# Inverse sums of the exponentials: turned once as 16 columns, stored to DRAM and loaded back spread over partitions; first T one slot later

## The chip, the cores and the metric

The kernel runs on one core of one Trainium2 chip. The metric is the device time of one execution in microseconds; lower is better. The profiler's times are microseconds from the start of the span unless marked ns. Its engines are PE (TensorE's matmuls), PEld (its weight loads), DVE (VectorE), ACT (ScalarE), POOL (GpSimd) and SP (SyncE, which issues the DMAs).

## The reference

A transformer block for 2048 tokens of 1024 features: a layer norm that is scaled and shifted by the row c, causal attention in four segments of 512 tokens with a running memory, an output projection, a second norm, and a gated feed-forward layer. The part that the change touches is the attention of one head (32 heads of 32 features):

```python
for s in range(N):                       # N = 4 segments of L = 512 tokens
    logits = einsum("bhqd,bhkd->bhqk", qs, ks) * scale + mask
    p = softmax(logits, axis=-1)
    a_dot = einsum("bhqk,bhkd->bhqd", p, vs)
    pq = phi(qs)
    num = einsum("bhld,bhde->bhle", pq, M)
    den = einsum("bhld,bhd->bhl", pq, z)[..., None] + 1e-6
    o = g * (num / den) + (1.0 - g) * a_dot
    M = M + einsum("bhld,bhle->bhde", phi(ks), vs)
    z = z + einsum("bhld->bhd", phi(ks))
```

The softmax divides by a sum of exponentials for each token and head, and the result is weighted with 1 − g. That factor, (1 − g) / sum, is what the change carries another way.

## The kernel before, in words

Everything is float32; projections are three products of rounded high and low parts. After a start of some 95 us the attention runs as 32 steps, one for each group of four heads (G = 8) and each segment, two segments of every group in a first half and two in a second. The feed-forward layer follows from some 1020 us on and is not touched.

The steps are pipelined in a loop (n from 0 to 32). Each loop is a list of slots, the string ORDER, in which every letter takes one piece of a generator: K (v and k of the next step: four pieces of v, then k, then the turns vT and kT), Q (q of the next step), S (scores of this step, query block by query block), A (sums of the running memory), M (what is read from the memory), V (the values of the step before), N (norm of later tokens, in the loops n = 1 to 9 or so). TensorE runs in exactly this order. DVE, ACT, POOL and SP are ordered by a scheduler with a cost model, and each of them then takes its instructions strictly in the order given.

For one step the work is:

- S: four products for each block of 128 queries, S (L498). DVE finds the row minimum of the negated scores (L500, mm) and ACT the exponentials with their sums (L502, ll). Then mt, a turn by DVE (tt, L513) and four writes into qs (L515) put the row maxima into the operand of the next product.
- the inverse sums: rc, 128 queries by 16 (four query blocks by four heads), is the reciprocal of ll (L519) times 1 − g (L520). ACT copies it to rx, with each value repeated over the 32 features of its head (L522).
- V: four key blocks. T(kc) is four products of keys with queries (L562), one for each head; ACT takes the exponentials pt (L564) and POOL sets what the mask excludes to zero (L565). PV(kc) sums them with the values vx into O (L571). The slots are T(0), T(1), PV(0) and PV(1), T(2), T(3), PV(2) and PV(3), then the end.
- the end: O holds features by tokens, so the factor must stand as features by tokens too. TensorE turns rx in four 128 x 128 blocks into the PSUM tile R (L585), ACT copies it (L589), DVE multiplies O with it (L590). Where a memory exists, ry is turned the same way (Y, L585) and added (L593). The result goes to DRAM (oT_d, L595).

PSUM has two buffers for projections (v, k and q in turn), five that S, T, num, R and Y share, and one for O. vr (L369) is the copy of v, kh (L384) the high part of k, eq, ql and pq come from q. na (L245) is the normalized row block of N, with mra (L243) and rsa (L238) ahead of it, and hta (L272) its turned and scaled form.

Of the kernel before, what the change touches and what calls it, by code (L numbers as in the profile page):

```python
# [19 lines left out]
P = 128  # L20
# [16 lines left out]
def block_kernel(ctx: ExitStack, tc: tile.TileContext, x, c, wmod, wq, wk, wv, wo, beta, wg, wu, wd, out):  # L37
# [10 lines left out]
    x1_d = dram.tile([T, D], F32, name="x1_d")  # L48
    mix_d = dram.tile([4 * L, L], F32, name="mix_d")
# [437 lines left out]
    def scores(n, g, s):  # L487
# [5 lines left out]
        for i in range(4):  # L493
            nk = max(256, (i + 1) * P)
            nv = (i + 1) * P
            for j in range(4):
                ps = s_ps(f"S{nm}_{j}{i}")
                nc.tensor.matmul(ps[:, :nk], qs[:96, j, i * P:(i + 1) * P], ks[:96, j, :nk], start=True, stop=True)  # L498
                sj = t2(f"sj{nm}_{j}{i}", "sj", bufs=3)
                nc.vector.tensor_tensor_reduce(out=sj[:, :nv], in0=ps[:, :nv], in1=mask[:, L - nv:], scale=-1.0,  # L500
                                               scalar=3.4e38, op0=ALU.add, op1=ALU.min, accum_out=mm[:, j, i:i + 1])
                nc.scalar.activation(sj[:, :nv], sj[:, :nv], AF.Exp, bias=mm[:, j, i:i + 1], scale=-1.0,  # L502
                                     accum_out=ll[:, i, j:j + 1])
            if i < 3:
                yield
# [14 lines left out]
        nc.vector.tensor_mul(rc, rc, omg[:, 4 * g:4 * g + 4].unsqueeze(1).to_broadcast([P, 4, 4]))  # L520
        rx = t2("rx" + nm, "rx", shape=(P, 4, 4, DH))
        nc.scalar.activation(rx, rc.unsqueeze(3).to_broadcast([P, 4, 4, DH]), AF.Copy)  # L522
        SC[n] = [rx, None]
# [25 lines left out]
    def values(n, g, s):  # L549
        nm = f"{g}_{s}"  # L550
        qs, ks, vx, pq = ST.pop(n)
        rx, ry = SC.pop(n)
# [21 lines left out]
        for kc in (0, 2):  # L574
            for k in (kc, kc + 1):
                T(k)
                yield
# [4 lines left out]
        def turned(r, name):  # L582
            ps = s_ps(name + nm)
            for i in range(4):
                nc.tensor.transpose(ps[:, i * P:(i + 1) * P], r[:, i].rearrange("p a b -> p (a b)"), ident)  # L585
            return ps

        rr = tmp_tile("R" + nm)
        nc.scalar.activation(rr, turned(rx, "R"), AF.Copy)  # L589
        nc.vector.tensor_mul(rr, po, rr)  # L590
        yield
        if s > 0:
            nc.vector.tensor_add(rr, rr, turned(ry, "Y"))  # L593
# [730 lines left out]
    ORDER = "K N K K V K V N K K V V K N V K S Q S V V Q S Q A S K M Q V V"  # L1324
# [6 lines left out]
    with tc.manual_schedule(engines={mybir.EngineType.PE}):  # L1331
# [27 lines left out]
        for n in range(len(steps) + 1):  # L1359
# [22 lines left out]
            if n == 30:  # L1382
# [5 lines left out]
                def cut(k):  # L1388
# [3 lines left out]
                         (22, lambda: get(2)), (32, lambda: cut(2)), (26, lambda: get(3)), (35, lambda: cut(3))]  # L1392
# [69 lines left out]
```

## Time and profile before

| what | value |
|---|---|
| time, median of three runs | 2802.66 us (2799.39 to 2803.0) |
| the profiled execution: time | 2800.21 us |
| its span, mean granted clock | 2798.5 us, 0.995 |
| TensorE busy in the span | 2727.7 us, 97% |
| attention loops, 100 to 1020 us | 920 us; PE 905.49, ACT 655.32, DVE 593.80, POOL 340.83 busy |
| share of the DMA engines in that stretch | 0.60, 132 GB/s |

A row of the windows gives, for a stretch, the busy time of each engine with its count of instructions in brackets. A row of the groups gives line, engine, operation, tiles and shapes, then the busy time and the mean ns of one, then the idle time of the engine just before them with what ended it. A row of the waits names who waited for what, with the total, the number and the longest. In the timeline a row is start, length, engine, line and a count of like instructions in a row; brackets hold the idle time before it. The chain of waits names the work that ended last at each moment.

### The profile page before, as it was taken

The numbers are of one execution on the slowest core, as the hardware profiler recorded it, in microseconds if no ns is written. First come the engines' busy times: TensorE is split into PE (matmuls) and PEld (weight loads), VectorE is DVE, ScalarE is ACT, GpSimd is POOL, SyncE is SP. The second block draws the span as 40 slices with busy tenths as digits, with TensorE's granted clock in tenths as the row PEclk, the third lists the DMA queues.
The fourth block names the chain that finished last, engine by engine and source line by source line (L and its number), as shares of the span: only waits on it lengthen the run. The fifth ranks groups of instructions, "written<-read, shape, count | busy, mean of one in ns | idle before, by whom it ended". The sixth has DMA issues, their size and how long they took to land.

```text
span 2798.5 us, 38460 instructions
## 1 busy us (share of the span) xinstructions
PE 2727.7 (97%) x13276; PEld 2207.4 (79%) x13276; DVE 1761.9 (63%) x3727; ACT 1291.8 (46%) x2861; POOL 540.9 (19%) x986
## 2 busy tenths in 40 slices
PE   5999999999999999999999999999999989999999
PEld 4777777777777777888888887888888878888887
DVE  7566566766666744677776768666777744334543
ACT  6688876767676735234343224222322243232220
POOL 0333334333332531100000002000000002112432
PEclk9999999999999999999999999999999999999999
DMA  7566655665555647655555644334576675544652
GB/s 228 129 148 137 159 113 127 149 140 125 116 115 99 144 171 242 202 207 211 214 205 186 243 177 152 127 137 151 188 250 246 248 259 168 182 143 153 206 187 79
DMA packets 229604, 480.17 MB, mean 172 GB/s; under 512 B 17440, under 2 KB 92192, under 8 KB 229408
## 3 DMA queue, kind: packets, MB, share of 16 engines
q1 hardware_dynamic: 229408, 477.72, 56.7%
q8 instruction: 104, 1.70, 0.3%
q14 instruction: 92, 0.75, 0.1%
HBM read 300.96 MB, written 126.35 MB: 153 GB/s over the span
## 4 chain that ended last, share of the span: by engine, by line
PE 87%; DVE 7%; issue 2%; DMA 2%; ACT 2%; POOL 1%; SPq 0%; DVEq 0%; ACTq 0%; POOLq 0%
PE f L1125 37%; PE d L1284 19%; PE k L365 6%; PE q L365 5%; PE y L630 5%; PE v L365 3%; PE S L498 3%; PE O L571 3%; PE T L562 3%; DVE qs L515 1%; PE M L478 1%; PE R L585 1%; DVE sj L500 1%; PE num L536 1%; PE vT L378 0%
## 5 line engine op out<-in xcount | busy, mean ns | idle before, releaser
L1125 PE MATMUL f<-A,B 128*128 128x512 f32 x4704 | 1074.6, 390 | 4.9 <-DVE c L1090 3.2
L1125 PEld LDWEIGHTS f<-A,B 128*128 128x128 f32 x4704 | 882.3, 188 | 190.5 <-issue 2.9
L1284 PE MATMUL d<-wb,ah 128*128 128x512 f32 x2352 | 536.0, 390 | 7.3 <-DVE wb L1174 3.8
L1284 PEld LDWEIGHTS d<-wb,ah 128*128 128x128 f32 x2352 | 442.3, 188 | 101.0 <-DVE wb L1174 4.9
L500 DVE CUSTOM_DVE_ANT_0 sj<-S,mask 128x384 f32<-128x384 f32 (+3 forms) x512 | 227.9, 487 | 183.9 <-PE S L498 175.3
L502 ACT ACTIVATE sj<-sj,mm 128x384 f32<-128x384 f32 (+3 forms) x512 | 282.4, 556 | 27.5 <-DVE mm L500 25.2
L564 ACT ACTIVATE pt<-T 128x256 f32<-128x256 f32 (+3 forms) x512 | 184.9, 455 | 119.9 <-PE T L562 119.2
L1174 DVE TENSOR_TENSOR ah<-ar,ah 128x1792 fp32r<-128x1792 f32 x56 | 115.9, 2070 | 183.9 <-ACT ah L1173 183.9
L565 POOL TENSOR_SCALAR_AFFINE_SELECT pt<-pt 128x128 f32<-128x128 f32 x512 | 165.7, 342 | 339.1 <-ACT pt L564 332.1
L1173 ACT ACTIVATE ah<-ar 128x1792 fp32r<-128x1792 f32 x56 | 95.3, 1702 | 275.5 <-PE d L1284 245.9
L1092 ACT ACTIVATE g<-g 128x512 f32<-128x512 f32 x56 | 35.4, 632 | 309.9 <-DVE g L1092 309.9
L201 POOL TENSOR_TENSOR w<-r,w 128x256 fp32r<-128x256 f32 x180 | 133.8, 774 | 162.4 <-ACT w L196 162.3
L763 DVE TENSOR_TENSOR B<-t,B 128x512 fp32r<-128x512 f32 x168 | 116.1, 691 | 56.4 <-ACT B L766 56.3
L1197 POOL TENSOR_TENSOR yo<-u,gbb 128x256 f32<-128x256 f32 x32 | 29.2, 937 | 559.0 <-DMA hid_d<-sc 556.8
L766 ACT ACTIVATE B<-t 128x512 fp32r<-128x512 f32 x168 | 105.5, 628 | 63.2 <-PE f L1125 59.7
L630 PE MATMUL y<-wo,hho 128*128 128x512 f32 x384 | 125.8, 393 | 0.0
L562 PE MATMUL T<-qs,ks 128*128 128x256 f32 (+2 forms) x512 | 114.5, 338 | 5.6 <-DVE qs L515 1.9
L562 PEld LDWEIGHTS T<-qs,ks 128*128 128x128 f32 x512 | 83.2, 188 | 45.6 <-issue 21.7
L1089 ACT ACTIVATE g<-f 128x512 f32<-128x512 f32 x56 | 33.5, 599 | 176.8 <-PE f L1125 176.8
L763 DVE TENSOR_TENSOR B<-rg,B 128x512 fp32r<-128x512 f32 x112 | 77.8, 695 | 53.0 <-ACT B L766 52.9
L498 PE MATMUL S<-ks,qs 96*128 96x256 f32 (+2 forms) x512 | 108.1, 332 | 1.2 <-DVE mm L500 1.2
L1215 POOL TENSOR_TENSOR xo<-xo,yo 128x256 f32<-128x256 f32 x64 | 69.6, 1115 | 195.5 <-DMA xo<-x_d 155.4
(232 smaller groups left out, 4338.3 us busy)
## 6 DMA issues: line engine op xcount, KB each, us to landing
ar<-hid_d SPq DMA_DIRECT2D x56, 896.0 KB, 5.2
rg<-wg SPq DMA_DIRECT2D x56, 512.0 KB, 4.6
ru<-wu SPq DMA_DIRECT2D x56, 512.0 KB, 5.5
hid_d<-g SPq DMA_DIRECT2D x56, 512.0 KB, 3.0
sc<-hid_d SPq DMA_DIRECT2D x56, 512.0 KB, 5.6
hid_d<-sc SPq DMA_DIRECT2D x56, 512.0 KB, 3.0
br<-wT_d SPq DMA_DIRECT2D x49, 512.0 KB, 5.9
qs<-qh SPq DMA_DIRECT2D x64, 256.0 KB, 4.8
```

The lines of the kernel that those rows point to most:

```text
L201: eng.tensor_sub(w[:, 1, k:k + 256], r[:, k:k + 256], f32(w[:, 0, k:k + 256]))
L365: nc.tensor.matmul(ps, w[:, a], b, start=(kt == 0 and a == 0 and b is hi), stop=(kt == KT - 1 and a == 1))
L498: nc.tensor.matmul(ps[:, :nk], qs[:96, j, i * P:(i + 1) * P], ks[:96, j, :nk], start=True, stop=True)
L500: nc.vector.tensor_tensor_reduce(out=sj[:, :nv], in0=ps[:, :nv], in1=mask[:, L - nv:], scale=-1.0, scalar=3.4e38, op0=ALU.add, op1=ALU.min ...
L502: nc.scalar.activation(sj[:, :nv], sj[:, :nv], AF.Exp, bias=mm[:, j, i:i + 1], scale=-1.0, accum_out=ll[:, i, j:j + 1])
L562: nc.tensor.matmul(ps[:, :nn], ks[:, j, kc * P:(kc + 1) * P], qs[:, j, L - nn:], start=True, stop=True)
L564: nc.scalar.activation(pt, ps[:, nn - n:nn], AF.Exp)
L565: nc.gpsimd.affine_select(pt[:, :P], pt[:, :P], pattern=[[1, P]], compare_op=ALU.is_ge, fill=0.0, base=0, channel_multiplier=-1)
L630: nc.tensor.matmul(ps, b[:, i * P:(i + 1) * P], w[:, a, g % 2], start=(g == 0 and a == 0 and b is hi), stop=(g == G - 1 and a == 1))
L763: eng.tensor_sub(dst[:, k], a[:, k], b[:, k])
L1125: nc.tensor.matmul(ps, B[m, i][:, a, kt * P:(kt + 1) * P], A[p, i, kt][b], start=(start and kt == 0 and a == 0 and b == 0), stop=(kt == 3 ...
L1284: nc.tensor.matmul(ps[t], ops[n][:, x, k, t * P:(t + 1) * P], b[:, y, kk % 2], start=(kk == 0 and x == 0 and y == 0), stop=(kk == 13 and x ...
```

## The change

Four things change. The inverse sums keep their 16 columns (in the order head, query block) and are no longer repeated by ACT. Right behind T(0), one turn by TensorE makes 16 rows of 128 of them; ACT copies these to 16 rows of the tile tt, and SP stores them to DRAM as 16 x 128 (rc_d, two in turn). Behind T(2), four DMAs load them back, each a row of 512 tokens repeated over the 32 partitions of a head, into the tile rr. DVE multiplies O with rr as before. The four turns and the copy at the end go; those of ry stay. The string ORDER is rearranged around T(0) and T(1), and in loop 30 the loads and cuts of two weight blocks of wo come earlier.

```diff
+    rc_d = [dram.tile([16, P], F32, name=f"rc{i}_d") for i in range(2)]
...
-                                     accum_out=ll[:, i, j:j + 1])
+                                     accum_out=ll[:, j, i:i + 1])
...
-        nc.vector.tensor_mul(rc, rc, omg[:, 4 * g:4 * g + 4].unsqueeze(1).to_broadcast([P, 4, 4]))
-        rx = t2("rx" + nm, "rx", shape=(P, 4, 4, DH))
-        nc.scalar.activation(rx, rc.unsqueeze(3).to_broadcast([P, 4, 4, DH]), AF.Copy)
-        SC[n] = [rx, None]
+        nc.vector.tensor_mul(rc, rc, omg[:, 4 * g:4 * g + 4].unsqueeze(2).to_broadcast([P, 4, 4]))
+        SC[n] = [rc, None, tt]
...
                 T(k)
+                if k == 0:
+                    ps = s_ps("R" + nm)[:16, :P]
+                    nc.tensor.transpose(ps, rc.rearrange("p a b -> p (a b)"), ident)
+                    rows = tt[:16]
+                    nc.scalar.activation(rows, ps, AF.Copy)
+                    nc.sync.dma_start(rc_d[n % 2], rows)
+                if k == 2:
+                    rr = t2("R" + nm, "rx")
+                    for j in range(4):
+                        nc.sync.dma_start(rr[32 * j:32 * j + 32], bass.AP(tensor=rc_d[n % 2].tensor, offset=rc_d[n % 2].offset + j * L,
+                                                                         ap=[[0, 32], [1, L]]))
                 yield
...
-        rr = tmp_tile("R" + nm)
-        nc.scalar.activation(rr, turned(rx, "R"), AF.Copy)
         nc.vector.tensor_mul(rr, po, rr)
...
-    ORDER = "K N K K V K V N K K V V K N V K S Q S V V Q S Q A S K M Q V V"
+    ORDER = "K N K K K V K N V K V V K N V K S Q S V V Q S Q A S K M Q V V"
...
-                         (22, lambda: get(2)), (32, lambda: cut(2)), (26, lambda: get(3)), (35, lambda: cut(3))]
+                         (16, lambda: get(2)), (24, lambda: cut(2)), (21, lambda: get(3)), (30, lambda: cut(3))]
```

TensorE in loop 25, from T(0) to the first product of O, before. A name's digits are the segment, then head and block.

```order
L562 MATMUL T_2_30_9805<-qs_2_9392,ks_174 128x512
L365 MATMUL v_2_9769<-hhh_4_0_6031,w_1_5_9536 128x512
...
L365 MATMUL v_2_9769<-hhh_4_1_6048,w_1_5_9536 128x512
L562 MATMUL T_2_01_9826<-qs_2_9392,ks_174 128x384
...
L365 MATMUL k_2_9846<-hhh_1_0_5781,w_1_5_9621 128x512
...
L365 MATMUL k_2_9846<-hhh_2_1_5880,w_1_5_9621 128x512
L378 MATMUL vT_2_9859<-ident,vr_2_9816 128x128 x4
L571 MATMUL O_2_9789<-pt_2_00_9792,vx_2_9103 32x512
```

The same place in the changed kernel:

```order
L366 MATMUL v_2_9769<-hhh_4_1_6050,w_1_5_9545 128x512
L561 MATMUL T_2_00_9800<-qs_2_9392,ks_176 128x512
...
L578 MATMUL R_2_9820<-ident,rc_2_9718 16x128
L366 MATMUL k_2_9830<-hhh_1_0_5770,w_1_5_9630 128x512
...
L561 MATMUL T_2_01_9837<-qs_2_9392,ks_176 128x384
...
L366 MATMUL k_2_9830<-hhh_2_0_5854,w_1_5_9630 128x512
...
L379 MATMUL vT_2_9863<-ident,vr_2_9795 128x128 x4
L570 MATMUL O_2_9799<-pt_2_00_9802,vx_2_9082 32x512
```

All of v now stands ahead of T(0), the first piece of k between T(0) and T(1), and one piece of k instead of two between T(1) and O.

ACT in loop 6, one of those with the norm of later tokens, before:

```order
L522 ACTIVATE rx_1_2738<-rc_1_2735 128x512
L196 ACTIVATE w_0_4_3035<-r_0_4_2880 128x1024
L564 ACTIVATE pt_1_00_2821<-T_1_00_2819 128x512
...
L369 ACTIVATE vr_1_2845<-v_1_2785 128x512
L245 ACTIVATE na_2563<-na_2563,mra_2800,rsa_2797 128x1024
L564 ACTIVATE pt_1_01_2851<-T_1_01_2849 128x384
...
L564 ACTIVATE pt_1_31_2866<-T_1_31_2864 128x384
L272 ACTIVATE hta_0_2870<-tpa_0_2869,modT 128x128 x4
```

And in the changed kernel:

```order
L370 ACTIVATE vr_1_2824<-v_1_2785 128x512
L563 ACTIVATE pt_1_00_2831<-T_1_00_2829 128x512
L563 ACTIVATE pt_1_10_2836<-T_1_10_2834 128x512
L246 ACTIVATE na_2572<-na_2572,mra_2800,rsa_2797 128x1024
L563 ACTIVATE pt_1_20_2841<-T_1_20_2839 128x512
L563 ACTIVATE pt_1_30_2846<-T_1_30_2844 128x512
L580 ACTIVATE tt_1_2728<-R_1_2849 16x128
L273 ACTIVATE hta_0_2861<-tpa_0_2860,modT 128x128 x4
L563 ACTIVATE pt_1_01_2875<-T_1_01_2873 128x384
```

vr stands ahead of the exponentials of T(0), na ahead of two of them, and the copy tt and four hta ahead of those of T(1). In every second one of these loops na stands behind all four exponentials of T(0).

DVE in loop 25, around the product with O, in the changed kernel (before, that product L590 stood between the first and the second reduce of the block of 384):

```order
L501 ISA sj_3_33_10049,mm_3_9940<-S_3_33_10047,mask 128x512
L501 ISA mm_3_9940 128x1
L592 TENSOR_TENSOR R_2_9897<-O_2_9799,R_2_9897 128x512
L509 CAST mt_3_10052<-mm_3_9940 128x16
L539 TENSOR_SCALAR dn_3_10089<-num_3_0_10083 128x8
L510 TENSOR_TENSOR mt_3_10052<-mm_3_9940,mt_3_10052 128x16
L539 TENSOR_SCALAR dn_3_10089<-num_3_1_10084 128x8
L514 STREAM_TRANSPOSE tt_3_10055<-mt_3_10052 32x32 x4
```

The product now stands behind the last reduce of S and ahead of mt and the turn.

More of the change, by code (lines that the diff above doesn't have):

```diff
@@ L551, in values @@
         qs, ks, vx, pq = ST.pop(n)
-        rx, ry = SC.pop(n)
+        rc, ry, tt = SC.pop(n)
         po = o_ps("O" + nm)
@@ L580, in values @@
             yield
[L582 to L586, printed above, removed]
-        rr = tmp_tile("R" + nm)
-        nc.scalar.activation(rr, turned(rx, "R"), AF.Copy)
         nc.vector.tensor_mul(rr, po, rr)
@@ L592, in values @@
         if s > 0:
-            nc.vector.tensor_add(rr, rr, turned(ry, "Y"))
+            ps = s_ps("Y" + nm)
+            for i in range(4):
+                nc.tensor.transpose(ps[:, i * P:(i + 1) * P], ry[:, i].rearrange("p a b -> p (a b)"), ident)
+            nc.vector.tensor_add(rr, rr, ps)
             yield
```

## The prediction

> **What bounds the kernel now.** First the page: the busy times of the engines and the chain of work that ended last.
>
> ```profile
> PE 2727.7 (97%) x13276; PEld 2207.4 (79%) x13276; DVE 1761.9 (63%) x3727; ACT 1291.8 (46%) x2861; POOL 540.9 (19%) x986
> PE 87%; DVE 7%; issue 2%; DMA 2%; ACT 2%; POOL 1%; SPq 0%; DVEq 0%; ACTq 0%; POOLq 0%
> ```
>
> TensorE is busy 97% of the span and holds 87% of the chain. The change lies in the attention loops alone, so I read the table of windows next, for the 32 loops that turn R (the first turn stands at 114.4, the last at 1008.4).
>
> ```profile
> 100.00:1020.00 920.00, 905.49 (x5226) 708.34 (x5226) 593.80 (x1978) 655.32 (x1854) 340.83 (x760) 1.00 0.60 132
> ```
>
> In these 920 us TensorE is busy 905.49, at a granted clock of 1.00; it sits idle 14.5 us. So the stage has two things to give: TensorE's own work, and at most 14.5 us of waits. ACT (655.32) and DVE (593.80) have slack as totals. What the waits are, the list of waits of PE in this window says (line waited for: us in total, times, longest):
>
> ```profile
> PE k L365 <- ACT vr L369: 3.4, 7, 0.5
> PE T L562 <- DVE qs L515: 1.9, 3, 0.8
> PE T L562 <- DVE ry L544: 1.8, 5, 0.4
> PE T L562 <- ACT pt L564: 1.4, 3, 0.8
> PE O L571 <- POOL pt L565: 1.2, 2, 1.0
> ...
> PE k L365 <- DVE pq L419: 0.7, 2, 0.3
> ```
>
> Four of these rows, k on vr, k on pq, T on qs and T on ry, are the ones that the new order touches: 3.4 + 0.7 + 1.9 + 1.8 = 7.8 us.
>
> **1. The four turns of R leave TensorE.** The timeline of PE around one of them (start, us, count), and the chain of waits at the same place with the turn of Y and one K slot:
>
> ```profile
> 802.30 0.86 PE L571 MATMUL O<-pt,vx 128*32 128x256 f32 x16
> 803.09 0.66 PE L585 MATMUL R<-ident,rx 128*128 128x128 f32 x4
> 803.50 0.48 PE L365 MATMUL q<-hhh,w 128*128 128x512 f32 x1
> 803.82 0.39 PE L365 MATMUL q<-hlh,w 128*128 128x512 f32 x1
> ```
>
> ```profile
> 798.64 1.39 PE k L365 x6
> ...
> 803.15 0.59 PE R L585 x4
> ...
> 811.43 0.44 PE Y L585 x4
> ```
>
> From R's start to the next q are 803.50 − 803.09 = 0.41 us, and that q takes 0.48 instead of 0.39, 0.09 more: 0.50 us for a loop. The chain puts 0.59 on it. 32 loops: −16.0 us by the first, −18.9 by the second. I take −16.0, since starts are recorded and ends are modelled.
>
> **2. One turn of 16 columns comes.** It is one matmul against the identity where there were four. A quarter of the chain's R row is 0.59 / 4 = 0.15 us, a quarter of its Y row 0.11; alone it can't cost more than a whole transpose by itself:
>
> ```profile
> L585 PE MATMUL R<-ident,rx x128: 272/273/330, 114.4 to 1008.4; 128*128 128x128 f32 x128
> L571 PEld LDWEIGHTS O<-pt,vx 128*32 128x32 f32 x1024 | 28.0, 109 | 38.8 <-issue 20.6 <-POOL pt L565 8.0 <-POOL hlh L224 0.2
> L585 PEld LDWEIGHTS R<-ident,rx 128*128 128x128 f32 x128 | 13.6, 142 | 7.0 <-DVE mm L500 5.2 <-issue 1.6 <-DVE hho L223 0.2
> ```
>
> So 32 x 0.15 = +4.8 us, between 32 x 0.11 = 3.5 and 32 x 0.273 = 8.7. Its weight load has 16 columns; the nearest row is the 32-column load of O at 109 ns, against 142 ns at 128 columns, so little of the load's cost goes away and I keep 0.15. [...]
>
> Terms 1 and 2 together: −11.2 us, from −18.9 + 3.5 = −15.4 to −16.0 + 8.7 = −7.3.
>
> **3. Copies and the product.** Two copies leave ACT in each loop and a small one comes; the product stays on DVE:
>
> ```profile
> L522 ACT ACTIVATE rx<-rc 128x512 f32<-128x512 f32 x31 | 19.5, 628 | 45.7 <-DVE rc L520 45.7
> L589 ACT ACTIVATE R<-R 128x512 f32<-128x512 f32 x32 | 18.5, 578 | 3.1 <-PE R L585 3.1
> L564 ACT ACTIVATE pt<-T 128x128 f32<-128x128 f32 x128 | 25.4, 288 | 14.6 <-PE T L562 13.9 <-POOL pt L565 0.6
> ```
>
> ACT loses 19.5 + 18.5 = 38.0 us and gains 32 x 0.29 = 9.3 (the 128-element exponential is the nearest row). With 265 us of slack in the stage that is worth nothing by itself. Its places count: rx stood ahead of the exponentials of T(0), and the copy of the turned R among those of S. I give it 0 here; part of it returns in term 4.
>
> **4. Waits that go.** T(0) moves one K slot back, 1.39 us by the row of k above. The waits of T on ry were 0.4 at most and those on qs 0.8 at most, less than that slot; so 1.9 + 1.8 go, unless the chain on DVE grows. It doesn't by count: the product R takes a place among the reduces of S, in a later one than before. The k that opens the new slot follows T(0) and its turn, and vr now stands ahead of T(0)'s exponentials on ACT, so 3.4 + 0.7 go as well, if v's copy (0.63) is over by the end of T(0), some 1.1 us. I take all 7.8; between 0 (each wait only moves) and all 14.5 that TensorE sits idle.
>
> **5. Waits that come.** In eight early loops the norm of later tokens runs beside the attention, and ACT takes its place in a queue. One of these loops, in the timelines of ACT and PE:
>
> ```profile
> 248.06 1.25 ACT L245 ACTIVATE na<-na,mra,rsa 128x1024 f32<-128x1024 f32 x1 [1.91 <-DMA qs<-ql]
> 249.21 1.61 ACT L564 ACTIVATE pt<-T 128x384 f32<-128x384 f32 x4
> 250.69 1.53 ACT L272 ACTIVATE hta<-tpa,modT 128x128 f32<-128x128 f32 x4
> ```
>
> ```profile
> 245.35 0.86 PE L562 MATMUL T<-qs,ks 128*128 128x384 f32 x4
> 249.73 0.66 PE L378 MATMUL vT<-ident,vr 128*128 128x128 f32 x4 [0.33 <-ACT pt L564]
> 250.32 1.81 PE L571 MATMUL O<-pt,vx 128*32 128x512 f32 x16
> ```
>
> na stood idle for 1.91 us, and the exponentials of T(1), whose products had begun at 245.35, came only behind it: ACT works in order. In the new order the queue between na and those exponentials gains the copy tt (0.29) and four hta (1.53). From na's end at 249.31: 249.31 + 0.29 + 1.53 + 1.61 = 252.7, and POOL's select of some 0.34 makes 253.1. O's last four products of this half want it about 1.7 into its 1.81, at 252.0: 1.1 us late. Where na stands ahead of two exponentials of T(0) as well, 1.03 more: 2.2. Over eight loops 1.1 gives 8.8 and 2.2 gives 17.6. But na itself comes sooner in half of them, since POOL's rsa now stands ahead of the selects; there I halve it: +7, between 0 and 17.6. In the other 24 loops ACT has, from the end of v, 0.63 (vr) + 2.06 + 0.29 + 1.61 = 4.6 us of work and POOL 0.34 behind it, 4.9; TensorE comes to the same exponentials after T(0) 1.07, the turn 0.15, a K slot 1.39, T(1) 0.86, a K slot 1.39, vT 0.44 and half of O 0.9, at 6.2. That is a cover of 1.3 us, so I set them at 0. The rows of ACT, PE and POOL that aren't above, the third that of a copy ahead of the exponentials of T(0) there:
>
> ```profile
> 788.86 2.06 ACT L564 ACTIVATE pt<-T 128x512 f32<-128x512 f32 x4
> 790.78 0.63 ACT L369 ACTIVATE vr<-v 128x512 f32<-128x512 f32 x1
> 787.85 0.60 ACT L416 ACTIVATE eq<-q 128x512 f32<-128x512 f32 x1 [2.69 <-DVE ql L411]
> 243.08 1.07 PE L562 MATMUL T<-qs,ks 128*128 128x512 f32 x4
> 794.03 0.44 PE vT L378 x4
> L565 POOL TENSOR_SCALAR_AFFINE_SELECT pt<-pt 128x128 f32<-128x128 f32 x512 | 165.7, 342 | 339.1 <-ACT pt L564 332.1
> ```
>
> **6. The round trip.** Per loop SP gets five more DMAs: one of 8 KB to DRAM and four loads of 64 KB. Nearest rows (KB each, median us to landing), SP's issue after the k copy, and the last reduce of S in that loop:
>
> ```profile
> ks<-kl SPq DMA_DIRECT2D x30, 256.0 KB, 6.8
> qs<-ql SPq DMA_DIRECT2D x30, 256.0 KB, 4.2
> hT_d<-hta SPq DMA_DIRECT2D x16, 256.0 KB, 2.6
> ...
> 800.69 1.21 SPq L395 DMA_DIRECT2D ks<-kh  x2
> ...
> 809.84 0.69 DVE L500 CUSTOM_DVE_ANT_0 sj<-S,mask 128x512 f32<-128x512 f32 x1
> ```
>
> The store follows T(0) at some 3 us and lands 2.6 to 6.8 us later, before k is copied. In nine of the loops the loads stand behind the first ks, in the others ahead of it; at some 0.6 us for an issue the last is out at 803.7 and lands at 807.9 (4.2) to 810.5 (6.8). The product R stands there behind the last reduce in five of the nine, which ends at 810.5, and up to three reduces sooner in the others. So it is just covered: cost 0, with 0 to 2.6 us to spare in the five. Behind the product on DVE are mt, the turn tt and qs, and T(0) waits for qs; behind the waiting loads on SP are ks, qs and weights, wanted only a loop later. If the cover is gone, each us past it costs up to a us of each of the nine loops, once T(0)'s own slot (1.39) is used up. [...]
>
> At the last attention loop but one, wo's loads and cuts go 5 to 8 slots earlier; O's waits on POOL there are 1.2 us in total, so I set this at 0 within ±1.2.
>
> **Sum.** −11.2 − 7.8 + 7 = −12.0. The profiled run took 2800.21 us, with a span of 2798.5: 2788.2. The three runs were 2799.39 to 2803.0 with their median 2.45 above the profiled one, so the profile lies in their lower half; I say 2788.
>
> **The rivals.**
>
> *A, the queue on ACT costs in full.* Term 5 at its upper end: −11.2 − 7.8 + 17.6 = −1.4, 2799. For it: the row of na, where exponentials waited behind it. Against: DVE and POOL bring na sooner in half the loops. [...]
>
> *B, the time comes back as waits.* The 0.35 us that terms 1 and 2 save in a loop only brings TensorE sooner to qs, which DVE's chain times; 7.8 us of waits grow by 11.2 instead of going. The change then does not do what it says: 2800. For it: T waits for qs and ry already. Against: these were 8 waits in 32 loops, and T(0) comes 1.39 later.
>
> *C, O waits for ACT in every loop: slower.* Between T(1) and O stand one K slot and vT where N, K, K and vT stood in the early loops and two K slots in the late ones. If ACT comes to vr 2.3 us after v ends (weight cuts or late exponentials of S ahead of it), the cover of 1.3 is gone and O waits 1.0 in the 24 loops, and term 5 is at its upper end: −11.2 − 7.8 + 17.6 + 24 = +22.6, 2823. Past 2808 it goes at 0.4 us for each of those loops, from 1.7 us of lateness on. For it: eq waited for ql on ACT just ahead of T(0)'s exponentials. Against: in the loop shown the exponentials of T(0) start at 788.86, and with rx gone from ahead of them they could start 0.63 sooner.
>
> *E, the load of R is late: slower.* In nine loops the last of the four loads lands 11.5 us after its issue at 803.7, 4.7 past the reduces; 1.39 is covered and 3.3 reach T(0): 9 x 3.3 = 30, 2788 + 30 = 2818. It decides at 10.4 us from the issue. For it: no row of this trace is a load that repeats one row over 32 partitions. Against: 6.8 is the slowest of the medians.
>
> *D, more waits go.* Terms 1 and 2 as taken, all 14.5 us of idling gone and nothing new: 2800.2 − 25.7 = 2774.5. Against: O on POOL and T on pt are not touched by the order.
>
> **How the numbers follow.** Forecast 0.55, D 0.15, A 0.09, B 0.07, C 0.09, E 0.05. About 0.2%, 5.6 us, is what a measurement of this kernel can tell from no change, counted from the median of 2802.66: faster means below 2797.1. Faster: forecast and D, 0.70. Same: A and B, 0.16. Slower: C and E, 0.14. The forecast's own range is 2777 to 2796 (net turns −15.4 to −7.3, waits some ±5). The range leaves out C, E and a little of D below 2772, and takes in A and B with the 2.45 us by which the runs lie above the profile: 2772 to 2804.
>
> **What would show it.** Turns: R's row must read 32 and not 128 matmuls, and TensorE's busy time in the stage fall by 10 to 15 us over the same loops. Waits: k on vr, T on qs and T on ry should be gone from the list, and waits of O or T(1) on pt stand in eight loops before 330 us, 1 us each. Round trip: the product R on DVE should show no idle time with a DMA as its releaser; if it does, E has begun. The prediction is wrong if PE's idle time in the stage grows by more than the 11.2 us of work that leaves it.

## The result: 1.3% slower, and the profile after

The changed kernel takes 2835.70 us (median of 4 runs, 2834.57 to 2838.28), beside 2802.83 for the kernel before on the same chip: a ratio of 1.0126, 95% interval [1.0113, 1.0138]. 12 to 15 us of gain were forecast and 33 us of loss came. The profiled execution took 2838.28 us, with a span of 2836.6 against 2798.5 before: 38.1 us more to explain. That is 5 us more than the medians differ by, since the profiled execution was the slowest of its four and the one before lay 2.6 us under its median.

The busy times and the chain of work that ended last, of the changed kernel:

```profile
PE 2732.3 (96%) x13180; PEld 2206.4 (78%) x13180; DVE 1772.2 (62%) x3727; ACT 1261.6 (44%) x2829; POOL 533.4 (19%) x986
PE 83%; DVE 8%; ACT 3%; DMA 3%; issue 2%; POOL 1%; SPq 0%; DVEq 0%; ACTq 0%; POOLq 0%
```

TensorE executes 96 matmuls fewer, 13180 against 13276, as the change says, and yet its share of the chain falls from 87% to 83%: DVE, ACT and DMA have taken a point each. The attention stage in the table of windows:

```profile
100.00:1020.00 920.00, 876.65 (x4967) 681.58 (x4967) 587.69 (x1943) 611.24 (x1787) 314.77 (x727) 0.99 0.61 132
```

In the same 920 us TensorE is now idle for 43.4 us instead of 14.5, at a granted clock of 0.99. That is 28.9 us more, where the prediction had called itself wrong from 11.2 on. What it waits for in the attention loops is in its list of waits, 100 to 1060 us (total, times, longest):

```profile
PE T L561 <- DVE qs L516: 7.5, 6, 2.9
PE k L366 <- ACT vr L370: 7.5, 8, 1.4
PE S L499 <- DVE mm L501: 6.1, 7, 2.4
PE num L535 <- DVE mm L501: 5.2, 5, 2.8
PE T L561 <- ACT tt L580: 4.7, 3, 2.2
PE O L570 <- POOL pt L564: 4.4, 3, 2.4
...
PE y L635 <- DVE xr L639: 3.0, 2, 1.5
```

Two of the four waits that were to go, k on vr and T on qs, have grown from 3.4 and 1.9 to 7.5 each. S and num wait for the row minima mm. All of them are few and long: not a price that each loop pays, but a few bad places.

**Where they are.** To find the places I read from PE's timelines the start of T(0) in every loop, in both kernels; the difference is the lag of the changed one. Loops 14 and 16 before:

```profile
474.43 0.97 PE L562 MATMUL T<-qs,ks 128*128 128x512 f32 x3 [0.46 <-DVE qs L515]
532.39 0.84 PE L562 MATMUL T<-qs,ks 128*128 128x512 f32 x3
```

And after:

```profile
499.36 0.84 PE L561 MATMUL T<-qs,ks 128*128 128x512 f32 x3
574.26 1.07 PE L561 MATMUL T<-qs,ks 128*128 128x512 f32 x4
```

The lag is 499.36 − 474.43 = 24.9 us in loop 14 and 574.26 − 532.39 = 41.9 in loop 16: two loops lose 17.0. The table gives the us that the lag grows by: "15–16" is from the T(0) of loop 14 to that of loop 16, which the first expectations call loops 14 and 15. The start-up before the first T(0) is left out of the reasoning, since it is −2.3 and +3.5 us in two kernels below whose first ten loops are those of before. Each kernel was profiled once; in the four kernels below that leave loops 2 to 10 as they were, that stage reads +0.8, +0.3, −0.5 and −0.4, so less than about 1 us tells nothing.

| stage | before the first T(0) | loops 2–10 | 11–14 | 15–16 | 17–30 | 31–32 | after | span |
|---|---|---|---|---|---|---|---|---|
| changed kernel | +5.7 | +18.3 | +0.9 | **+17.0** | **−9.7** | +9.6 | −3.7 | +38.1 |

So one long stage does gain, about 0.7 us a loop from loop 17 to 30. The loss lies in three others.

**Loops 15 and 16.** The normed rows of the later tokens are read back from DRAM there: rh (L214), which DVE and POOL split into hhh and hlh. All eight of these loads, in the kernel before:

```profile
L213 SPq DMA_DIRECT2D rh<-hT_d x8: 377/405/537, 420.0 to 506.6; - x8
```

And in the changed kernel:

```profile
L214 SPq DMA_DIRECT2D rh<-hT_d x8: 370/414/486, 501.0 to 539.0; - x8
```

They are issued from 420 on in the one, spread over 87 us, and within 38 us from 501 on in the other: the first 81 us later, of which the lag is only 25. It stands in loop 12 before and in loop 14 after. SP is not short of time: its issues take 15 of the 60 us from 440 to 500. It is the order that SP was given. Its queue before, the first two loads of rh with what follows (ks and qs are the operands of the steps, the first digit the segment):

```order
L421 DMA qs_0_5023<-ql_0_5020 32x4x512
L213 DMA rh_0_5741<-hT_d 128x2x512
L213 DMA rh_1_5750<-hT_d 128x2x512
L395 DMA ks_175<-kh_1_5188 32x4x512 x2
...
L98 DMA r_1_0_5758<-wv 128x1024
L395 DMA ks_174<-kh_0_5540 32x4x512 x2
```

And in the changed kernel:

```order
L396 DMA ks_176<-kh_0_5549 32x4x512
L585 DMA R_0_5512<-rc_d 32x512 x4
L396 DMA ks_176<-kh_0_5549 32x4x512
...
L422 DMA qs_0_5729<-qh_0_5725 32x4x512
L600 DMA oT_d<-R_0_5512 128x512
L214 DMA rh_0_5741<-hT_d 128x2x512
L214 DMA rh_1_5750<-hT_d 128x2x512
L99 DMA r_1_0_5758<-wv 128x1024
```

The scheduler used to place the loads of rh ahead of two steps' ks (kh_1_5188 and kh_0_5540). With four loads of R in every loop it places them behind both, where they are written in the program; those of weights (r_1_0) likewise. The rows land late and their splits fall among the reduces of S. DVE there:

```profile
519.63 0.98 DVE L224 CAST hhh<-rh 128x512 fp32r<-128x512 f32 x1 [0.34 <-DMA rh<-hT_d]
520.64 1.10 DVE L225 TENSOR_TENSOR hlh<-rh,hhh 128x512 fp32r<-128x512 f32 x1
521.66 0.94 DVE L224 CAST hhh<-rh 128x512 fp32r<-128x512 f32 x1
522.52 0.54 DVE L501 CUSTOM_DVE_ANT_0 sj<-S,mask 128x384 f32<-128x384 f32 x1
```

Three splits, 3 us, stand ahead of the reduce of S. PE behind it, and at the T(0) that follows:

```profile
523.13 0.50 PE L499 MATMUL S<-ks,qs 96*128 96x512 f32 x1 [2.44 <-DVE mm L501]
534.32 1.21 PE L561 MATMUL T<-qs,ks 128*128 128x512 f32 x4 [2.94 <-DVE qs L516]
```

S waits 2.44 for a buffer and T(0) 2.94 for qs. A second cost comes on top, in the windows of these two loops, from the T(0) of loop 14 to that of loop 16, before and after:

```profile
474.43:532.39 57.96, 55.84 (x325) 44.09 (x325) 43.74 (x142) 38.71 (x114) 23.40 (x47) 1.00 0.69 155
499.36:574.26 74.90, 64.06 (x320) 47.52 (x318) 52.58 (x149) 39.71 (x113) 29.78 (x54) 0.91 0.67 160
```

TensorE's idle time grows from 2.1 to 10.8 us, 8.7 more, and its busy time from 55.8 to 64.1, 8.2 more, for about as many matmuls at a granted clock of 0.91 instead of 1.00. Together that is the 17.0 of the lag. Read in pieces, the clock of the changed kernel is 0.89 from 520 to 540 us, 0.87 from 540 to 575 and 1.00 from 575 to 600. The longest wait of TensorE in the two loops is 2.94 us; what brought the clock down is not shown.

**Loops 2 to 10.** The eight loops with the norm. ACT in one of them:

```profile
288.54 1.06 ACT L197 ACTIVATE w<-r 128x1024 fp32r<-128x1024 f32 x1 [3.44 <-DMA r<-wq]
289.98 0.59 ACT L370 ACTIVATE vr<-v 128x512 f32<-128x512 f32 x1
...
294.01 1.24 ACT L246 ACTIVATE na<-na,mra,rsa 128x1024 f32<-128x1024 f32 x1 [1.49 <-DVE mra L244]
295.16 0.25 ACT L580 ACTIVATE tt<-R 16x128 f32<-16x128 f32 x1
295.32 1.46 ACT L273 ACTIVATE hta<-tpa,modT 128x128 f32<-128x128 f32 x4
```

And PE:

```profile
290.63 0.50 PE L366 MATMUL k<-hha,w 128*128 128x512 f32 x1 [1.14 <-ACT vr L370]
...
295.46 0.45 PE L561 MATMUL T<-qs,ks 128*128 128x384 f32 x1 [2.22 <-ACT tt L580]
```

Two chains are seen. A weight (r<-wq, loaded by SP) comes late, ACT stands 3.44 us at its cut, vr is late and k waits 1.14. SP issued that load at 281.31, and in the kernel before at 254.64: 26.7 us later, of which 15.7 are the lag of this loop. And the copy tt stands behind na: it holds the PSUM tile that T(1) wants, which waits 2.22.

**Loops 31 and 32.** Here the output projection y begins beside the last loops. Its operand ro, the rows that the attention stored in oT_d, is loaded and split as rh is. Before and after:

```profile
L213 SPq DMA_DIRECT2D ro<-oT_d x16: 359/374/548, 846.8 to 1048.7; - x16
L214 SPq DMA_DIRECT2D ro<-oT_d x16: 370/383/444, 936.8 to 1091.0; - x16
```

The first load stands in loop 27 before and in loop 29 after, 90.0 us later, of which 34.4 are the lag. Work on ro (a split of 1.55 us at 985.27, then a product of 1.21 for the weights) stands on DVE ahead of a reduce of S at 988.21, and num waits for that:

```profile
988.95 0.82 PE L535 MATMUL num<-mz,pq 128*128 128x132 f32 x4 [2.83 <-DVE mm L501]
```

### The profile page after: what moved, and what is told of

Same layout as the page of the kernel before. It is cut to its first block, busy times and chain, and to the rows that moved or that the text cites. A ratio compares the mean times of both kernels' runs of the same rounds, so it can differ in the third digit from the quotient of the medians.

```text
span 2836.6 us, 38415 instructions
## 1 busy us (share of the span) xinstructions
PE 2732.3 (96%) x13180; PEld 2206.4 (78%) x13180; DVE 1772.2 (62%) x3727; ACT 1261.6 (44%) x2829; POOL 533.4 (19%) x986
## 4 chain that ended last, share of the span: by engine, by line
PE 83%; DVE 8%; ACT 3%; DMA 3%; issue 2%; POOL 1%; SPq 0%; DVEq 0%; ACTq 0%; POOLq 0%
PE f L1130 36%; PE d L1289 19%; PE k L366 6%; PE y L635 5%; PE q L366 4%; PE v L366 3%; PE T L561 3%; PE O L570 3%; PE S L499 2%; ACT sj L503 1%; DVE qs L516 1%; DVE sj L501 1%; POOL w L202 1%; PE num L535 1%; PE vT L379 0%
```

## The experiments

Theories are named by letters in the expectations. Q: the new order, through ACT's queue. T: the turn with its store and loads. L: the loads on SP push its other loads back. W: ACT's queue in the early loops carries nearly all. B: bandwidth, or an R that lands late. O: the new order where rh is split. (The rivals A to E of the prediction are another list.) Lags are in us by stage, as in the table above; ratios are to the kernel before on the same chip. The diffs are shortened, with conditions written out.

### Halves of the change

**The order alone.** The kernel before, with the new string only:

```diff
-    ORDER = "K N K K V K V N K K V V K N V K S Q S V V Q S Q A S K M Q V V"
+    ORDER = "K N K K K V K N V K V V K N V K S Q S V V Q S Q A S K M Q V V"
```

> The kernel before with the new order of slots alone: four turns of R as before, no store and no load, wo's loads at their old slots. The trace after lags by 18 us over loops 1 to 8, 17 us over loops 14 and 15, 10 us at the end, and gains 10 us over loops 16 to 28. Theory Q (the new order puts the norm's na and hta ahead of T(1)'s exponentials on ACT): the 18 us of the early loops come with the order alone, so 2815 to 2825. Theory T (the turn with its store and loads is what delays, through SP and through tt on ACT): at or below the kernel before, 2795 to 2805.

2821.50 us, 1.0067 [1.0052, 1.0082]. Loops 2–10 +9.6, 15–16 +0.5, 17–30 +6.7, 31–32 +2.0. The order costs in the early loops, as theory Q said, and by itself in the late ones too, which it had not said.

**The turn alone.** The changed kernel with the old string and wo's old slots:

```diff
-    ORDER = "K N K K K V K N V K V V K N V K S Q S V V Q S Q A S K M Q V V"
+    ORDER = "K N K K V K V N K K V V K N V K S Q S V V Q S Q A S K M Q V V"
...
-                         (16, lambda: get(2)), (24, lambda: cut(2)), (21, lambda: get(3)), (30, lambda: cut(3))]
+                         (22, lambda: get(2)), (32, lambda: cut(2)), (26, lambda: get(3)), (35, lambda: cut(3))]
```

> The changed kernel with the old order of slots and wo's loads at their old slots: the turn of 16 columns, the store and the loads alone. Theory Q: the early loops are as before and TensorE keeps its 11 us, though loops 14 and 15 may still lose: 2790 to 2810. Theory T: most of the loss stays, 2820 to 2835.

2832.03 us, 1.0107 [1.0092, 1.0122]. Loops 2–10 +4.2, 15–16 +16.2, 17–30 +1.8, 31–32 +10.8. The losses at the two bad places belong to the turn with its DMAs, whatever the order. But from 17 to 30 neither half gains, and both together do. The twelve loops 18 to 29, from T(0) to T(0), in the windows of the kernel before, the order alone, the turn alone and the changed kernel:

```profile
588.82:931.70 342.88, 337.63 (x1950) 263.93 (x1949) 224.66 (x770) 237.09 (x681) 121.25 (x277) 1.00 0.56 114
603.38:953.56 350.18, 344.21 (x1949) 265.77 (x1948) 225.50 (x771) 238.83 (x681) 115.74 (x277) 1.00 0.55 114
616.21:959.29 343.08, 335.26 (x1914) 259.50 (x1912) 223.58 (x770) 224.59 (x668) 116.38 (x277) 1.00 0.59 124
631.31:963.90 332.59, 329.94 (x1914) 260.41 (x1912) 223.19 (x769) 225.63 (x668) 115.70 (x277) 1.00 0.61 128
```

What TensorE waits for there with the turn alone:

```profile
PE T L569 <- DVE ry L551: 3.0, 9, 0.6
PE T L569 <- DVE R L612: 2.4, 2, 2.0
PE T L569 <- DVE qs L519: 2.0, 5, 1.1
```

With the old order the turn takes 2.4 us from TensorE's busy time (337.63 − 335.26), and idling grows from 5.3 to 7.8: T(0) arrives sooner and waits for ry, qs and R. That is the prediction's rival B, shown for these loops. With the new order alone idling hardly changes (6.0), but the busy time grows by 6.6. It hides a wait: in every second loop from 20 to 28 the sixteen products of O take some 3.5 us instead of 1.71. One of these loops, PE and POOL:

```profile
782.18 3.48 PE L578 MATMUL O<-pt,vx 128*32 128x512 f32 x16
780.98 1.43 POOL L205 TENSOR_TENSOR w<-r,w 128x256 fp32r<-128x256 f32 x2 [0.66 <-ACT w L200]
782.37 0.29 POOL L572 TENSOR_SCALAR_AFFINE_SELECT pt<-pt 128x128 f32<-128x128 f32 x1
782.62 0.73 POOL L205 TENSOR_TENSOR w<-r,w 128x256 fp32r<-128x256 f32 x1
```

POOL's cuts of a weight w stand among the selects of pt that O wants, and the rows of O put 1.6 us of this loop on those selects. In the changed kernel POOL's eight selects follow one another there and O takes 1.71 in each of the twelve loops; busy time falls by 7.7 and idling to 2.6. Why the scheduler puts w there in the one and not in the other is not shown.

**The old slots of wo.** The changed kernel with the second part of the diff above.

> The changed kernel with wo's loads and cuts back at their old slots in loop 30. If the 10 us lost from loop 29 on come from these earlier loads and cuts, 2825 to 2829; if they come from the order or the round trip, 2834 to 2838.

2828.29 us, 1.0092 [1.0077, 1.0107]. The time is the one expected if wo were the cause, but by stage it is the changed kernel (+16.7, +16.7, −9.8, +10.3): wo's slots are not the cause of the loss at 31–32, and the time hit by chance. Of the 7.2 us between the two spans 3.0 are the start-up (+2.7 instead of +5.7) and 3.0 lie between T(0) of loop 32 and the feed-forward layer (170.6 instead of 173.6).

**Only where it pays.** Turn and order in loops 16 to 28, wo's old slots:

```diff
-                if k == 0:
+                if k == 0 and 15 <= n <= 27:
...
-            for pos, q in enumerate((ORDER if n else ORDER0).split()):
+            for pos, q in enumerate(((ORDER if 16 <= n <= 28 else OLD) if n else ORDER0).split()):
```

> The new order and the turn with its round trip in loops 16 to 28 alone (no norm, no loads of the normed rows, no wo there), the rest as before. In the trace after these 13 loops run 9.6 us shorter than before. If that gain is theirs and not paid for elsewhere, 2790 to 2795, faster than both kernels; if it is only time that loops 14 and 15 had put off, 2800 to 2805.

2794.39 us, 0.9972 [0.9962, 0.9981]: faster than the kernel before. Loops 17–30 −11.2, 31–32 +4.5, the other loops within 1.4. The change pays where no norm and no load of rh stands beside it.

### The loads

**Without the loads.** A resident tile stands in for R:

```diff
-                    for j in range(4):
-                        nc.sync.dma_start(rr[32 * j:32 * j + 32], bass.AP(...))
...
-        nc.vector.tensor_mul(rr, po, rr)
+        nc.vector.tensor_mul(rr, po, mask[:, :L])
```

> The changed kernel without the four loads of R; O is multiplied with a constant tile instead, so the inverse sums are left out of the output. The turn, the copy and the store stay. Theory L (the loads keep SP's other loads from being placed a loop earlier: the normed rows rh of loops 14 and 15, wo's weights at the end): most of the 17 us of loops 15 and 16 and of the 10 us at the end goes, 2806 to 2818. Theory W (the early loops' queue on ACT carries nearly all): 2826 to 2836.

2797.86 us, 0.9983 [0.9972, 0.9995]: below the range of theory L. The loads cost 2835.70 − 2797.86 = 37.8 us (36.5, each taken against the kernel before on its own chip), more than the whole loss. Loops 2–10 +5.9, 15–16 +1.2, 17–30 −10.0, 31–32 +0.9. The loads of rh stand early again (430.0 to 513.8, from loop 12 on), and those of ro too (from 847.1 on, in loop 27).

**Neither store nor loads.** As above, with the store gone too.

> The changed kernel without the store and without the loads; the turn and its copy stay, O is multiplied with a constant tile, so the inverse sums are left out of the output. Theory L: loops 15 and 16 and the end lose nothing any more, the early loops lose what the order alone costs (10 us), and loops 17 to 29 keep their gain of 10: 2798 to 2810. If the DMAs matter little, 2825 to 2836.

2795.28 us, 0.9970 [0.9959, 0.9981]. Loops 2–10 +7.4, 15–16 −1.4, 17–30 −9.0, 31–32 −0.4: much like the kernel without the loads, and again below the range. The store costs little.

**Loads that wait for no store.** They read a table in DRAM that is stored once, in the first step:

```diff
+                    if n == 0:
+                        nc.sync.dma_start(rc_d[2], rows)
...
-                        nc.sync.dma_start(rr[32 * j:32 * j + 32], bass.AP(tensor=rc_d[n % 2].tensor, ...))
+                        nc.sync.dma_start(rr[32 * j:32 * j + 32], bass.AP(tensor=rc_d[2].tensor, ...))
```

> The changed kernel with the loads of R taken from a table that is stored once in the first step, so that no later load waits for its step's store; inverse sums of other steps are left out of the output. If SP loses by waiting for the store to land (36 us of such waits in the trace after), the loops 15 and 16 recover: 2810 to 2822. If it is the place of the loads in SP's order and not the wait, 2828 to 2838.

2827.46 us, 1.0091 [1.0057, 1.0124], of two runs 6.5 us apart, about where it was expected if the place of the loads counts and not the wait. Loops 15–16 +14.2 and 31–32 +9.0 stay: there it is not that loads wait for their store with SP's queue behind them. Loops 2–10 fall from +18.3 to +10.7: there it is, in part. Loops 17–30 gain 5.1 instead of 9.7.

**One load of four.** Only the first 64 KB, and the resident tile again:

```diff
-                    for j in range(4):
+                    for j in range(1):
```

> The changed kernel with the first of the four loads alone, 64 KB on SP's queue, and O multiplied with a constant tile, so the inverse sums are left out of the output. In SP's order the normed rows stand early again with this one load. Theory L as an order: 2797 to 2808. If any load on SP that follows the store does the harm, 2820 or more.

2795.02 us, 0.9971 [0.9960, 0.9982], a little below the range of theory L. Loops 2–10 +6.2, 15–16 +3.8, 17–30 −10.4, 31–32 −0.1; rh from 426.0 to 510.3. One load per loop, behind the same store, leaves the places of rh and ro (from 845.4 on) nearly as they were; four don't.

### The copy and the queues

**The copy on DVE.**

```diff
-                    nc.scalar.activation(rows, ps, AF.Copy)
+                    nc.vector.tensor_copy(rows, ps)
```

> The changed kernel with the copy of the 16 turned rows on DVE instead of ACT. T(1) waited 4.7 us for this copy in three early loops, since it holds R's slot in PSUM and stood behind na and the exponentials on ACT. Theory Q: those 4.7 us go and T(1)'s exponentials start 0.25 us sooner, 2827 to 2833. If DVE's own queue delays the copy as much, 2834 to 2840.

2827.86 us, 1.0092 [1.0063, 1.0121], in the range of theory Q. Loops 2–10 +11.3 instead of +18.3, the others as in the changed kernel (+12.9, −9.1, +10.4). The place of tt behind na costs 7 us. That is the same size as with the table, and the two may be one: a late copy makes a late store, for which the loads wait in SP's queue (in the changed kernel 16 times from 100 to 1060 us, 36.3 us in all and 5.1 at the longest). This link was not tried by itself. Theory W falls: of the 17.0 the copy's place on ACT can explain 4, and of the 9.6 nothing.

**The loads on ACT's queue.**

```diff
-                        nc.sync.dma_start(rr[32 * j:32 * j + 32], bass.AP(...))
+                        nc.scalar.dma_start(rr[32 * j:32 * j + 32], bass.AP(...))
```

> The changed kernel, complete, with the four loads of R issued from ACT's queue instead of SP's. In the order written for SP the loads of weights and of the normed rows rh then stand as early as without the loads. Theory L as an order (the loads harm because SP's queue puts the others behind them): the 37 us go except for what four issues cost on ACT, 2797 to 2808. Theory B (the 256 KB of a loop slow the other transfers, or R lands late): 2825 to 2836 again.

2825.92 us, 1.0080 [1.0059, 1.0100]: the time is in the range of theory B and far from that of L. The stages say otherwise. Loops 15–16 fall to +3.4 and 31–32 to +2.4, with the same bytes loaded, so theory B falls there. But loops 2–10 stay at +14.9, and 17–30 turn from −9.7 to +7.8. ACT in a late loop:

```profile
793.59 0.31 ACTq L593 DMA_DIRECT2D R<-rc_d  x1
793.94 1.38 ACTq L593 DMA_DIRECT2D R<-rc_d  x3
795.42 0.79 ACT L571 ACTIVATE pt<-T 128x128 f32<-128x128 f32 x4 [1.21 <-POOL pt L572]
```

The four issues take 1.7 us in ACT's order between the exponentials of T(2) and T(3), and ACT stands still for 1.21 (the profile names a select of POOL as what ended that, but the last issue ends only 0.1 us earlier). S then waits for its reduces 33 times, about once a loop, by the list of waits of the same kernel, for 14.2 us in all (0.8 us and two times before).

**The same, with the early loops left as before.** Turn from step 10, order from loop 11, wo's old slots, loads on ACT:

```diff
-                if k == 2:
+                if k == 2 and n >= 10:
```

> As the run with the loads on ACT's queue, but the old order and the old four turns up to loop 10, and wo's loads at their old slots: the early loops, where the order costs 6 to 10 us, stay as before, and loops 11 to 32 gain some 13 us as they did without the loads. 2787 to 2793, faster than both kernels; with theory B 2805 or more.

2807.66 us, 1.0019 [1.0009, 1.0028], not the 2787 to 2793 expected. Loops 2–10 +0.3, 15–16 +1.8, 17–30 +6.2, 31–32 +2.5. The losses of the early loops are gone with the change there; the issues on ACT still eat the gain.

**The same on POOL's queue.**

```diff
-                        nc.scalar.dma_start(rr[32 * j:32 * j + 32], bass.AP(...))
+                        nc.gpsimd.dma_start(rr[32 * j:32 * j + 32], bass.AP(...))
```

> As the run with the old order and old turns up to loop 10 and the loads on ACT's queue after it, which lost 0.3 to 1.0 us in every loop since four issues of some 0.43 us stood ahead of S's exponentials on ACT; here the loads are issued from POOL's queue, with SP's order as early as before. If it was ACT's time that ate the gain, loops 17 to 29 gain 9 us again and 15 and 16 lose little: 2788 to 2796. If POOL's issues hold its selects ahead of O instead, 2800 to 2815.

2802.71 us, 1.0002 [0.9993, 1.0012], again not the gain expected; the profiled execution, at 2798.32, is one of the fastest of ten. Loops 15–16 +0.6, 31–32 +2.9, 17–30 −4.8: loops 24 to 29 gain 1.0 each, and loops 18 to 23 lose part of it. It is not the selects that POOL's issues hold up there: O takes 1.71 in each of these loops. What else costs it is not shown.

### The loads while rh is due

What was still to be separated: is it the loads of R that spoil loops 15 and 16, or the new order of slots at the place where rh is split?

**A gap.** The changed kernel, with the old four turns and no DMA for R in steps 10 to 14:

```diff
-                if k == 0:
+                if k == 0 and not 10 <= n <= 14:
...
-                if k == 2:
+                if k == 2 and not 10 <= n <= 14:
```

> The changed kernel, but steps 10 to 14 (whose values are worked in loops 11 to 15) keep the old four turns, so no store and no loads stand in SP's order while the normed rows rh are due; the new order of slots and wo's slots as changed. Theory L (the loads on SP push the loads of rh, ks and weights out by a loop): the issues of rh lie spread again, the last before 530, and loops 15 and 16 lose less than 5 us instead of 17; the rest as in the changed kernel, so about 2818. Theory O (the loss of loops 15 and 16 is a matter of where the new order of slots meets the splits of rh, and any loads only add to it): loops 15 and 16 still lose 12 or more and the time is 2830 or above.

2820.64 us, 1.0068 [1.0054, 1.0082], where theory L had said 2818. Loops 15–16 fall to +0.4, and the other stages stay: 2–10 +16.4, 17–30 −10.2, 31–32 +12.5. Its loads of rh, and the window from its T(0) of loop 14 to that of loop 16:

```profile
L217 SPq DMA_DIRECT2D rh<-hT_d x8: 372/464/552, 453.4 to 527.3; - x8
```

```profile
496.12:554.52 58.40, 56.37 (x326) 44.34 (x324) 44.98 (x144) 38.90 (x113) 22.81 (x46) 1.00 0.64 145
```

rh is spread again over 74 us, the first load in loop 12; TensorE is idle for 2.0 us in the two loops instead of 10.8, and its clock is 1.00 instead of 0.91. The new order of slots stands in these loops all the same: it was not the order. The gap takes out turn, store and loads together; that it is the loads among them, the two kernels without loads say.

**Two queues.** Turn and order in loops 11 to 28, the loads on POOL's queue while rh is due and on SP's after, the old kernel elsewhere:

```diff
-                        nc.sync.dma_start(rr[32 * j:32 * j + 32], bass.AP(...))
+                        (nc.gpsimd if n < 15 else nc.sync).dma_start(rr[32 * j:32 * j + 32], bass.AP(...))
```

> The turn in steps 10 to 27 and the new order of slots in loops 11 to 28, old order, old turns and wo's old slots elsewhere; the four loads on POOL's queue for steps 10 to 14 and on SP's from 15 on. Theory L: with no load on SP while rh is due, its loads stay early and loops 11 to 16 lose nothing; loops 17 to 29 gain as in the changed kernel (10 to 11 us); about 2790, and faster than the kernel that changed loops 16 to 28 alone (2794). If loops 11 to 16 lose 5 us or more, the early stage doesn't bear the change even with the loads off SP, and it comes to 2795 or above.

2791.12 us, 0.9964 [0.9950, 0.9977]: the fastest of all, by median 3.3 us under the kernel that changes loops 16 to 28, though the two intervals overlap. Loops 11–14 −2.4, 15–16 +0.6, 17–30 −12.7, 31–32 +4.5. Its attention stage:

```profile
588.00:920.00 332.00, 329.77 (x1914) 259.94 (x1913) 223.16 (x769) 227.08 (x670) 117.32 (x278) 1.00 0.62 130
```

The twelve loops 18 to 29 take 11.6 us less than before (T(0) of loop 18 to that of loop 30: 589.0 to 920.3, against 588.8 to 931.7), with TensorE idle for 2.2.

All sixteen kernels side by side give the same answer, by the loop (from its T(0) to the next) in which the first load of rh and of ro is issued:

| first load | in loop | kernels | growth of the lag |
|---|---|---|---|
| rh | 12 | before and ten others | at 15–16: −1.4 to +3.8 |
| rh | 14 | changed, turn alone, old wo, table, copy on DVE | at 15–16: +12.9 to +17.0 |
| ro | 27 | before and seven others | at 31–32: −0.4 to +2.9 |
| ro | 29 | changed, turn alone, old wo, table, copy on DVE, gap, loops 16 to 28, two queues | at 31–32: +4.5 to +12.5 |

So the +4.5 of the two faster kernels at 31 and 32, where the old order and the old turns stand again, goes with loads of ro that come two loops late (from 893 on).

## Why the prediction was wrong, point by point

**The step that failed** is the sentence of term 6: "behind the waiting loads on SP are ks, qs and weights, wanted only a loop later". It looked at what stands behind the new loads in one loop of the stage from 17 on. It did not ask where the *other* loads on SP stand once these are in the list: a scheduler orders that queue, and rh and the weights had been placed up to two loops ahead of their need. They lost that lead. Where this term had put 0, the kernel without the loads is 37.8 us faster: some 16 at loops 15 and 16 (17.0 against 1.2), 9 at 31 and 32 and 12 in loops 2 to 10. That the loads cause it is shown by taking them away altogether and by leaving one of four; the gap and the table of rh and ro bear it out. No run forced the old order of SP's queue with the four loads in it. Why four of 64 KB push the scheduler's choices back and one doesn't is not shown; its model of a load's time is the likely reason, and stays an argument.

**Terms 1 and 2, the turns** (−16.0 and +4.8): right, read as the forecast read them. PE after, around the new turn:

```profile
824.93 0.27 PE L578 MATMUL R<-ident,rc 128*16 128x128 f32 x1
825.01 0.50 PE L366 MATMUL k<-hhh,w 128*128 128x512 f32 x1
825.35 0.40 PE L366 MATMUL k<-hlh,w 128*128 128x512 f32 x1
```

From R's start to the next k are 0.08 us, and that k takes 0.50 instead of 0.40: 0.18 for the turn, where 0.15 was forecast, so 0.32 a loop saved where 0.35 was. With the turn alone the busy time falls by only 0.20 a loop (2.4 over 12). Its waits of T are a likely reason, not one that was shown: in the kernel before, the T(0) of 787.33, with a wait in it, is busy 0.61 + 0.89 = 1.50 us, and that of 759.00, without one, 1.07.

**Term 3, ACT's copies** at 0: right in the late loops. In the early ones it is the place of tt that costs, which belongs to term 5.

**Term 4, the waits that go** (−7.8 for 32 loops): right where nothing else disturbs, though not by the order alone. In the twelve loops idling falls from 5.3 to 2.6, 0.2 a loop, about the 7.8 / 32. With the order alone k on vr (2.8 to 0.4) and T on ry (1.4 to none) do go, but k waits 3.3 for pq instead. The whole gain of terms 1, 2 and 4 was to be 19 / 32 = 0.59 a loop. In loops 22 to 28 of the changed kernel TensorE waits for nothing, and each is 0.95 to 1.26 us shorter: the forecast had spread over 32 loops waits of 0.34 to 0.46 that stood in each of these seven. With the disturbed loops it is 0.7 a loop in the changed kernel, and 0.81 in loops 11 to 28 of the version with two queues (14.5 over 18).

**Term 5, the queue on ACT in eight loops** (+7, up to 17.6): right in kind and size for the order, +9.6 with the order alone and +5.9 to +7.4 without the loads. With the order alone T(1) waits for pt in four of the early loops (0.86 to 1.44) and vT for ACT's hta in three (1.1 each). What it lacked is again what the loads do there: the late weight ahead of vr, and the late store.

**The shift of wo** at 0 ± 1.2: nothing changes with the old slots up to loop 32, and behind it the old slots are 3.0 us quicker in one profile each; more than the 1.2, but not measured by itself.

**The rivals.** A came true in the early loops and is the smaller part. B is what the turn gives with the old order. C did not come: its waits of O for ACT in every loop are not in the list (O waits 4.4 in all, for POOL, in three places). With the order alone its kin came, in every second late loop and by way of POOL. E had the right culprit and the wrong mechanism: a load of R lands 5.1 us after its issue at most, by the rows of its line, and the product with O waits for TensorE alone.

```profile
L592 DVE TENSOR_TENSOR R<-O,R x32: 677/685/692, 125.2 to 1050.8; 128x512 f32<-128x512 f32 x32
its engine sat idle before it (us, times) until:
  PE O L570: 4.7, 1
```

```profile
L585 SPq DMA_DIRECT2D R<-rc_d x128: 311/419/1479, 117.7 to 1037.8; - x128
...
DMA to landing us min/median/max: 2.0/3.4/5.1
```

The median of 3.4 us lies below the 4.2 to 6.8 that the prediction took from its nearest rows.

**What stays open:** why the scheduler gives SP and POOL these orders; which of the late loads costs how much in loops 2 to 10, and the link there between late copy and late weights; and what takes part of the gain in loops 18 to 23 with the loads on POOL.

## What to carry to other kernels

When a change adds transfers to an issuing queue whose order a scheduler makes, compare the whole queue before and after, and above all the place of the loads that are not part of the change: most of the cost here was not the new transfers' time, but the lead that others lost. A lost lead need not cost anything: in the changed kernel a load of wv that SP issued at 704.72 before, in loop 22, is issued at 797.88, in loop 24, and the loops there gain. It costs where what was loaded then stands in an engine's queue ahead of work that TensorE waits for: here three splits of rh, 3 us on DVE, ahead of a reduce for which S waited 2.44. Read the gain by stage, through the start of one recurring instruction in every loop; a total of +33 hid a gain of 10 and a loss of 17 in two loops. And read busy time with care: with the order alone TensorE's idle time hardly grew in the twelve loops (6.0 us instead of 5.3), since the waits lay between products of O that count as busy (3.48 us instead of 1.71 in the loop shown). A change that pays in one stage can then be made in that stage alone, and it turned from 1.0126 to 0.9964.

## What the hardware showed

The weight load of 16 columns takes 88 ns, beside 109 for the 32 columns of O and 142 for the 128 of the old turns; an eighth of the columns takes 0.62 of the time. Its row, with that of the loads' issues, from the rows of the tile R of the changed kernel:

```profile
L585 SPq DMA_DIRECT2D R<-rc_d x128: 311/419/1479, 117.7 to 1037.8; - x128
L578 PEld LDWEIGHTS R<-ident,rc x32: 86/88/90, 105.0 to 1033.4; 128*16 128x16 f32 x32
```

Issuing a load of R takes 0.42 us on SP (the median of those 128), 0.43 on ACT and 0.50 on POOL (medians of its rows there); four of them, 1.7 to 2.0 us, are more in the queue of a busy engine than the 0.35 us that the turn had to give. And the waits in loops 15 and 16 did not come alone: 8.7 us more of idling stand beside 8.2 us more of busy time, at a granted clock of 0.91 instead of 1.00.
